# In the eighth attention iteration, the first column pair's fill is issued behind the eight transposes

## The chip, the core and the metric

The kernel runs on one core of one Trainium2 chip. The metric is the device time of one execution in microseconds. All times in this document are in microseconds unless marked otherwise. The engines are TensorE (PE, with its weight loads shown apart as PEld), VectorE (DVE), ScalarE (ACT), GpSimd (POOL) and SyncE (SP, which here only issues DMAs).

## What is computed

The reference is a block of linear attention with a learned feature map, followed by a token-mixing MLP, for one sequence of 2048 tokens and 512 channels. Cut to what matters:

```python
h  = x + attention(layernorm(x))            # 32 heads of 16
h2 = h + mixer(layernorm(h))

# attention: pq, pk = per-head linear maps of q and k
phi_q = concat(softmax(pq), softmax(-pq));  phi_k = likewise
kv = phi_k^T v;  z = sum over tokens of phi_k
o  = (phi_q kv) / (phi_q z + 1e-6);  result = o @ wo

# mixer: works across the 2048 tokens, for every channel
u = gelu(h^T @ w1 + b1)                     # w1: 2048 x 1792
y = u @ w2 + b2                             # w2: 1792 x 2048
```

## The kernel before

The 2048 tokens are 16 tiles of 128. Products that need more than the matmul's own precision are made from three matmuls (`mm3`, L65 to L67): high part by high part, high by low, low by high. `split` (L60, L61) makes such a pair: ScalarE writes the high part, and another engine subtracts it from the source to get the low part.

The first stage makes k, v and q for all tiles. The stage around the change is a loop of 20 iterations, `for it in range(NT + 4)`, that runs the second half of the attention as a pipeline over token tiles. In it the order on TensorE, VectorE, ScalarE and GpSimd is the order in which the code is written, since a manual schedule is in force; only the SP queue's DMAs are placed by the planner, from estimated times. After the loop, until the last stage, the planner also orders the compute engines. What an iteration does, with names and lines:

- `s_pq(it + 1)` (GpSimd, L465) scales the next tile's exponentials `eq` by their weights `w`, which VectorE has made (`s_den`, L456 to L462). `s_ez(it + 3)` (GpSimd, L447) multiplies a later tile's exponentials by `zB`.
- `s_tr(it)` transposes the tile's `eq` with eight TensorE instructions (L532) into the PSUM tile `tn`, which has a single buffer, and ScalarE copies `tn` to `pht` in two halves (L534).
- `s_num`, in even iterations, takes two transposed tiles through `kvB` (L551), also into `tn`; ScalarE and VectorE make the parts `oh` (L557) and `ol` (L562) of it.
- `s_wo(it - 2)` is the output projection, four times `mm3` into `po`. `s_h(it - 2)` (VectorE, L579) adds the residual.
- `s_hn` (ScalarE L593 and L595, then `split`: L60 on ScalarE, L61 on GpSimd) normalizes a tile of the result into `HN`, tile `hs`. `s_rstd` (GpSimd, L590) makes the scale for a later tile. In iteration `it`, `s_hn(it - 4)` is issued: at it = 6 tile 2, at it = 7 tile 3.

TensorE has room in this loop, and the first layer of the mixer is begun in it. The 1792 columns of `w1` are taken in seven column pairs of 256. `fill(p)` adds one token tile to the sums of pair `p`: two times `mm3`, six matmuls into `pu`, the second and fifth of which read the low part of `HN`. Pairs 0 and 1 are filled in the loop by `fills(it)`, pair 1 first. In it = 7 pair 1 takes token tile 1 and pair 0 token tile 2. The weights come in pieces of two token tiles by `fill_load`: a DMA, a high part from ScalarE (L614), and a low part that is put in a list; `flush` has VectorE make the low parts of the list (L606). `flush` is called at the end of each iteration, ahead of that iteration's `fill_load` calls, in which pair 0 comes before pair 1.

In odd iterations the order on TensorE is: the fills, the eight transposes, the output projection. On ScalarE an odd iteration has the two evictions of `tn` ahead of `s_hn`.

After the loop come the remaining fills, the GELUs, and the second mixer layer (L834, L838), which combines blocks of `u` and `w2` into seven products for each step.

Of the kernel before, what the change touches and what calls it, by code (L numbers as in the profile page):

```python
# [28 lines left out]
V_NOT = (0, 1, 11)  # L29
SUMS = 8  # L30
LAG = 5
WARM = 9
EPS = 1e-5

# [2 lines left out]
def block_kernel(ctx: ExitStack, tc: tile.TileContext, x, xT, wT, phic, wo, w1, b1, w2, b2,  # L37
# [25 lines left out]
    def mm3(o, ah, al, bh, bl, first, last):  # L63

        nc.tensor.matmul(o, ah, bh, start=first, stop=False)  # L65
        nc.tensor.matmul(o, ah, bl, start=False, stop=False)  # L66
        nc.tensor.matmul(o, al, bh, start=False, stop=last)  # L67
# [92 lines left out]
    def negate():  # L160

        if MN:
            ev, mx, mn = MN.pop(0)
            nc.gpsimd.tensor_sub(mn, mn, mx)
            nc.gpsimd.tensor_sub(ev[:, :, 1], mn.unsqueeze(3).to_broadcast([P, NPR, 2, DH]), ev[:, :, 0])
# [5 lines left out]
    def run(*lists):  # L171
        for op in turns(*lists):
            op()
# [49 lines left out]
    with tc.tile_pool(name="prep", bufs=1) as prep:  # L223
# [67 lines left out]
        warm = ps_k.tile([P, P], F32, name="pk_ps", tag="pk_ps")  # L291
        for _ in range(WARM):
            nc.tensor.matmul(warm, ones, ones, start=True, stop=True)
# [72 lines left out]
    def q_mm():  # L366
        if q["mm"] < NT:
            PS[q["mm"]] = proj(q["mm"], wqh, wql, ps_q, "pu")
            q["mm"] += 1

    def q_logits(lag):
        n = q["logits"]
        if n < min(NT, q["mm"] - lag + NT * (q["mm"] == NT)):
            EQ[n] = big.tile([P, NG, P], F32, name="eq", tag="big")
            q["logits"] += 1
            return logit_ops(PS[n], EQ[n], n >= len(Q_AT))
        return []

    def q_exp(lag):
        n = q["exp"]  # L380
        if n < min(NT, q["logits"] - len(MN) - lag):
            exps(n, EQ[n])
            q["exp"] += 1
# [61 lines left out]
    def s_ez(t):  # L445
        EZ[t] = az.tile([P, NG, P], F32, name="ez")
        nc.gpsimd.tensor_mul(EZ[t], EQ[t], zB)  # L447

    def s_den(t):


        tz = az.tile([P, NPR, 2, 2], F32, name="tz")
        den = az.tile([P, NPR, 2], F32, name="den")
        W[t] = az.tile([P, NPR, 2, 2], F32, name="w", bufs=3)
        other = SQ[t]
        return [lambda: nc.vector.reduce_sum(tz.rearrange("p g c h -> p (g c h)"), heads(EZ[t]), axis=AX.X),  # L456
                lambda: nc.vector.scalar_tensor_tensor(tz[:, :, 0], other[:, :, 1], 1e-6, tz[:, :, 0],
                                                       op0=ALU.mult, op1=ALU.add),
                lambda: nc.vector.tensor_mul(tz, other, tz),
                lambda: nc.vector.reduce_sum(den, tz.rearrange("p g c h -> p g h c"), axis=AX.X),  # L460
                lambda: nc.vector.reciprocal(den, den),
                lambda: nc.vector.tensor_mul(W[t], other, den.unsqueeze(2).to_broadcast([P, NPR, 2, 2]))]  # L462

    def s_pq(t):
        nc.gpsimd.tensor_mul(heads(EQ[t]), heads(EQ[t]), W[t].rearrange("p g c h -> p (g c h)").unsqueeze(2).to_broadcast([P, 2 * H, DH]))  # L465
# [60 lines left out]
    def s_tr(t):  # L526
        j, i = divmod(t, 2)
        if i == 0:
            PHT[j] = ak.tile([P, NG, 2, P], F32, name="pht", bufs=1)
        ptr = ps_t.tile([P, 2, 4, P], F32, name="tn")  # L530
        for g in range(NG):
            nc.tensor.transpose(ptr[:, g // 4, g % 4, :], EQ[t][:, g, :], ident)  # L532
        for half in range(2):
            nc.scalar.activation(PHT[j][:, half * 4:half * 4 + 4, i, :], ptr[:, half], AF.Copy)  # L534

    def s_kv():

        pt = ps_o.tile([P, 2, P], F32, name="po")
        for b in range(2):
            nc.tensor.transpose(pt[:, b, :], kvS[:, 2 * b:2 * b + 2, :].rearrange("p n f -> p (n f)"), ident)  # L540
        nc.scalar.activation(kvB, pt, AF.Copy)

    def s_num(j):


        pn = ps_t.tile([P, 2, 4, P], F32, name="tn")
        for b in range(2):
            for c in range(4):
                for r in range(2):
                    rows, cols = slice(64 * r, 64 * r + 64), slice(32 * c, 32 * c + 32)  # L550
                    nc.tensor.matmul(pn[cols, r, 2 * b:2 * b + 2, :], kvB[rows, b, cols], PHT[j][rows, 4 * b + c, :, :],  # L551
                                     start=True, stop=True, skip_group_check=True)
        oh = ak.tile([P, 2, 2, 2, P], F32R, name="oh", bufs=1)
        ol = ak.tile([P, 2, 2, 2, P], F32R, name="ol", bufs=1)
        pv = pn.rearrange("p r (b i) s -> p i r b s", i=2)
        for i in range(2):
            nc.scalar.activation(oh[:, i], pv[:, i], AF.Copy)  # L557
        OS[j] = oh, ol, pv

    def s_ol(j):  # L560
        oh, ol, pv = OS[j]
        return [lambda i=i: nc.vector.tensor_sub(ol[:, i], pv[:, i], oh[:, i]) for i in range(2)]  # L562
# [8 lines left out]
    def s_x(t):  # L571
        HT[t] = ak.tile([P, D], F32, name="h", bufs=4)
        nc.sync.dma_start(HT[t], x[t * P:(t + 1) * P, :])
# [18 lines left out]
    def s_hn(t):  # L592
        nc.scalar.activation(VE[t][:, 1:2], VE[t][:, 1:2], AF.Copy, scale=r2[:, t:t + 1])  # L593
        hn = ak.tile([P, D], F32, name="hn")
        nc.scalar.activation(hn, HT[t], AF.Identity, scale=r2[:, t:t + 1], bias=VE[t][:, 1:2])  # L595
        HN[t] = big.tile([P, 2, D], F32R, name="hs", tag="big")
        split(HN[t][:, 0], HN[t][:, 1], hn, nc.gpsimd)
# [5 lines left out]
    def flush():  # L603
        while LATER:
            wl_, raw, wh_ = LATER.pop(0)
            LO.append(nc.vector.tensor_sub(wl_, raw, wh_).ins)  # L606
# [15 lines left out]
    def fill_load(p):  # L622
        if FL[p] < NT:
            WI[p, FL[p]] = stream(w1v, FL[p], 2, p * 256, 256)
            FL[p] += 2

    def fill(p, pool=None):

        t = FN[p]
        FN[p] = t + 1  # L630
        if FL[p] <= t:
            fill_load(p)
        if any(part is WI[p, t - t % 2][1] for part, _, _ in LATER):
            flush()
        if t == 0:
            PU[p] = [pool.tile([P, D], F32, name="pu", tag="pu") for _ in range(2)]
        a, b = WI[p, t - t % 2]
        for c in range(2):
            mm3(PU[p][c], a[:, t % 2, c * P:(c + 1) * P], b[:, t % 2, c * P:(c + 1) * P],
                HN[t][:, 0], HN[t][:, 1], t == 0, t == NT - 1)  # L640

    def fills(it):
        if FN[1] < it - LAG:
            fill(1, ps_q)
        if FN[0] <= it - LAG:
            fill(0, ps_f)

    for it in range(NT + 4):
        even = it % 2 == 0
        if 0 <= it + 1 < NT:  # L650
            s_pq(it + 1)
        if it == 0:
            s_tr(0)
            s_kv()
        if it == 1:
            run(q_logits(0))
            q_mm()
            s_tr(1)
        if it > 1 and even and it <= NT:
            s_num(it // 2 - 1)  # L660
        den = s_den(it + 2) if it + 2 < NT else []
        if it > 1 and even and it <= NT:
            ol = s_ol(it // 2 - 1)
            run(ol[:1] + den[:1] + ol[1:])
            den = den[1:]
        if it < NT:
            s_x(it)
        if it + 3 < NT:
            s_ez(it + 3)
        negate()  # L670
        q_mm()
        fills(it)
        q_exp(0)
        logits = q_logits(1)
        if it >= 4 and even:
            s_hn(it - 4)
        if 3 <= it < NT + 3 and even:
            s_moments(it - 3)
        if it > 1 and even and it - 2 < NT:
            s_wo(it - 2)  # L680
        if 1 < it < NT:
            s_tr(it)
        if it > 1 and not even and it - 2 < NT:
            s_wo(it - 2)
        if it >= 4 and not even:
            s_hn(it - 4)
        if 3 <= it < NT + 3 and not even:
            s_moments(it - 3)
        if 3 <= it < NT + 3:
            s_rstd(it - 3)  # L690
        run(logits + (q_sums(0) if it > 0 else []), den)
        if it > 0:
            negate()
        if not logits:
            flush()
        if 0 <= it - 2 < NT:
            s_h(it - 2)
        flush()
        for p in range(2):
            if it >= LAG - 3 + p and FL[p] <= FN[p] + 2 * (FN[p] > 0):  # L700
                fill_load(p)
# [276 lines left out]
```

## Time and profile before

| | us |
|---|---|
| median of 3 runs | 523.35 (523.15 to 523.65) |
| the profiled execution's own time | 523.61 |
| its span, first to last instruction | 521.8 |
| TensorE busy in the span | 515.2 |
| VectorE, ScalarE, GpSimd busy | 386.0, 282.0, 239.6 |
| granted TensorE clock | 1.000 of full |

A row of a timeline gives the start, the duration, the engine, the source line, the operation, what it writes and reads, shapes and a count; in square brackets, if the engine stood idle before, how long and what released it. Neighbouring instructions of the same kind are merged into one row, whose duration then reaches from the first start to the last end. A matmul's duration contains overlap with its neighbours: while TensorE runs without a break, matmuls of 512 columns start 0.23 apart though each lasts 0.39. Registers, branches and semaphore instructions are not counted as work.

### The profile page before, as it was taken

How to read it: one execution, taken by the hardware profiler on the slowest of the kernel's cores; microseconds unless marked ns; L12 is line 12 of the kernel's file. 1: busy time of each engine (PE TensorE's matmuls, PEld its weight loads, DVE VectorE, ACT ScalarE, POOL GpSimd, SP SyncE). 2: the span in 40 equal slices, each digit the busy share in tenths (PEclk: the TensorE clock that was granted, in tenths of full speed). 3: DMA queues.
4: the chain of work that ended last, by engine and by line, in shares of the span. 5: the costliest groups of instructions: out<-in, count | busy, mean ns of one | idle time of the engine just before them, and what ended most of it. 6: DMA issues, size and time to landing. Idle time of an engine off the chain costs nothing.

```text
span 521.8 us, 8917 instructions
## 1 busy us (share of the span) xinstructions
PE 515.2 (99%) x3379; PEld 435.8 (84%) x3379; DVE 386.0 (74%) x681; ACT 282.0 (54%) x496; POOL 239.6 (46%) x188
## 2 busy tenths in 40 slices
PE   8999999999999999999999999999999999999997
PEld 7888888887877767887788888888889999999997
DVE  6893999986899998773227423725869899988985
ACT  5999853435246876666956423625553424434430
POOL 2479799985999999874425000000002112112220
PEclk9999999999999999999999999999999999999999
DMA  8644211021041324344323354532215686678734
GB/s 299 200 131 121 75 41 38 1 69 36 21 122 49 96 98 125 118 125 137 103 85 118 102 162 155 168 100 82 62 59 109 164 190 147 130 170 180 166 49 81
DMA packets 36298, 58.52 MB, mean 112 GB/s; under 512 B 3744, under 2 KB 19360, under 8 KB 36256
## 3 DMA queue, kind: packets, MB, share of 16 engines
q1 hardware_dynamic: 31936, 51.37, 31.5%
q0 software_dynamic: 4032, 6.42, 9.7%
q8 instruction: 26, 0.43, 0.4%
q10 hardware_dynamic: 288, 0.17, 0.1%
q14 instruction: 16, 0.13, 0.1%
HBM read 46.81 MB, written 11.14 MB: 111 GB/s over the span
## 4 chain that ended last, share of the span: by engine, by line
PE 89%; POOL 7%; DVE 2%; DMA 1%; issue 1%; SPq 0%; ACT 0%; POOLq 0%
PE py L834 16%; PE pu L65 12%; PE pu L66 12%; PE pu L67 11%; PE py L838 10%; PE pv L66 3%; PE pv L67 3%; PE pv L65 3%; PE pk_ps L65 2%; PE pk_ps L67 2%; PE pk_ps L66 2%; POOL ez L447 2%; POOL eq L465 2%; PE po L66 2%; PE po L65 2%; PE po L67 2%
## 5 line engine op out<-in xcount | busy, mean ns | idle before, releaser
L66 PE MATMUL pu<-hs,whi 128*128 128x512 f32 x224 | 87.7, 391 | 1.1 <-POOL hs L61 1.1
L65 PE MATMUL pu<-hs,whi 128*128 128x512 f32 x224 | 87.5, 395 | 0.0
L67 PE MATMUL pu<-hs,wlo 128*128 128x512 f32 x224 | 87.1, 390 | 0.0
L606 DVE TENSOR_TENSOR wlo<-wraw,whi 128x512 fp32r<-128x512 f32 x56 | 43.7, 784 | 53.2 <-ACT whi L614 53.0
L899 POOL DMA_DIRECT2D out<-ot x7 | 6.2, 885 | 151.1 <-DVE ot L895 151.1
L796 ACT ACTIVATE whi<-wraw 128x1792 fp32r<-128x1792 f32 x28 | 47.4, 1701 | 46.0 <-DVE wraw L787 19.8
L805 DVE TENSOR_TENSOR wlo<-wraw,whi 128x1792 fp32r<-128x1792 f32 x28 | 56.5, 2021 | 11.7 <-PE py L838 9.4
L614 ACT ACTIVATE whi<-wraw 128x512 fp32r<-128x512 f32 x56 | 34.9, 628 | 49.6 <-PE pu L66 45.3
L65 PEld LDWEIGHTS pu<-hs,whi 128*128 128x128 f32 x224 | 42.1, 188 | 10.7 <-issue 2.5
L66 PEld LDWEIGHTS pu<-hs,whi 128*128 128x128 f32 x224 | 42.1, 188 | 10.4 <-POOL hs L61 2.1
L834 PE MATMUL py<-uf,whi 128*128 128x512 f32 x175 | 49.8, 395 | 0.0
L67 PEld LDWEIGHTS pu<-hs,wlo 128*128 128x128 f32 x224 | 42.1, 188 | 8.7
L447 POOL TENSOR_TENSOR ez<-eq,zB 128x1024 f32<-128x1024 f32 x16 | 38.3, 2398 | 4.4 <-ACT zB L494 4.4
L838 PE MATMUL py<-uf,whi 128*128 128x256 f32 x210 | 39.1, 283 | 0.0
L200 POOL TENSOR_TENSOR pk<-pk,sk 128x1024 f32<-128x1024 f32 x16 | 31.0, 1940 | 7.6 <-DVE sk L199 5.1
L534 ACT ACTIVATE pht<-tn 128x512 f32<-128x512 f32 x32 | 17.4, 595 | 30.2 <-PE tn L532 30.2
L465 POOL TENSOR_TENSOR eq<-eq,w 128x1024 f32<-128x1024 f32 x16 | 32.2, 2015 | 1.3 <-DVE w L462 1.3
L838 PEld LDWEIGHTS py<-uf,whi 128*128 128x128 f32 x210 | 32.8, 192 | 0.0
L834 PEld LDWEIGHTS py<-uf,wlo 128*128 128x128 f32 x175 | 28.5, 189 | 5.0
L61 POOL TENSOR_TENSOR hs<-hn,hs 128x512 fp32r<-128x512 f32 x16 | 21.6, 1349 | 23.7 <-ACT hs L60 23.7
L204 POOL TENSOR_TENSOR zacc<-zacc,pk 128x1024 f32<-128x1024 f32 x13 | 31.3, 2405 | 0.6
L834 PEld LDWEIGHTS py<-uf,whi 128*128 128x128 f32 x175 | 29.1, 190 | 2.7
(179 smaller groups left out, 1331.9 us busy)
## 6 DMA issues: line engine op xcount, KB each, us to landing
wraw<-in_w SPq DMA_DIRECT2D x56, 256.0 KB, 2.8
wraw<-in_w SPq DMA_DIRECT2D x28, 512.0 KB, 4.4
xraw<-in_xT SPq DMA_DIRECT2D x16, 256.0 KB, 3.0
xh<-in_x SPq DMA_DIRECT2D x16, 256.0 KB, 2.7
h<-in_x SPq DMA_DIRECT2D x16, 256.0 KB, 2.7
out<-h SPq DMA_DIRECT2D x16, 256.0 KB, 2.6
out<-ot POOLq DMA_DIRECT2D x14, 256.0 KB, 4.7
wraw<-in_wT SPq DMA_DIRECT2D x12, 256.0 KB, 5.2
```

Of the source, the lines that this page charges most:

```text
L65: nc.tensor.matmul(o, ah, bh, start=first, stop=False)
L66: nc.tensor.matmul(o, ah, bl, start=False, stop=False)
L67: nc.tensor.matmul(o, al, bh, start=False, stop=last)
L204: nc.gpsimd.tensor_add(zacc, zacc, PK[t])
L447: nc.gpsimd.tensor_mul(EZ[t], EQ[t], zB)
L465: nc.gpsimd.tensor_mul(heads(EQ[t]), heads(EQ[t]), W[t].rearrange("p g c h -> p (g c h)").unsqueeze(2).to_broadcast([P, 2 * H, DH]))
L606: LO.append(nc.vector.tensor_sub(wl_, raw, wh_).ins)
L614: nc.scalar.activation(wh_, raw, AF.Copy)
L796: nc.scalar.activation(WH[g], RAW[g], AF.Copy)
L805: nc.vector.tensor_sub(wl_, RAW[g], WH[g])
L834: nc.tensor.matmul(o, w, u, start=p == 0 and not low, stop=p == NP - 1, skip_group_check=True)
L838: nc.tensor.matmul(bank[bk][:, half], AW[sp, p][x][:, a], UB[p, b][:, y], start=p == 0 and half == 0 and i == 0, stop=p == NP - 1 and i == ...
```

## The change

Only in the iteration with it = 7 (`BEHIND`), the fill of pair 0 is not issued in `fills` but behind `s_tr`. TensorE's order there becomes: the fill of pair 1, the eight transposes, the fill of pair 0, the output projection. All other iterations keep their order.

```diff
+BEHIND = 7
...
-    def fills(it):
+    def fills(it, both):
         if FN[1] < it - LAG:
             fill(1, ps_q)
+        if both:
+            fill_last(it)
+
+    def fill_last(it):
         if FN[0] <= it - LAG:
             fill(0, ps_f)
...
-        fills(it)
+        fills(it, it != BEHIND)
         q_exp(0)
...
         if 1 < it < NT:
             s_tr(it)
+        if it == BEHIND:
+            fill_last(it)
         if it > 1 and not even and it - 2 < NT:
             s_wo(it - 2)
```

## The prediction

> **What bounds the kernel now.** I read the page first, then the list of waits of TensorE over the whole span, then the timeline of each engine around the eighth iteration of the attention loop (it = 7), and last the timeline of older places where VectorE and GpSimd had met in the same way.
>
> ```profile
> span 521.8 us, 8917 instructions
> PE 515.2 (99%) x3379; PEld 435.8 (84%) x3379; DVE 386.0 (74%) x681; ACT 282.0 (54%) x496; POOL 239.6 (46%) x188
> ...
> PE 89%; POOL 7%; DVE 2%; DMA 1%; issue 1%; SPq 0%; ACT 0%; POOLq 0%
> ```
>
> TensorE is busy for 99% of the span, and it is 89% of the chain that ended last. So what counts is whether TensorE gets through its list sooner; a faster engine beside it is worth something only where TensorE waits for it. The waits of TensorE (waiter, waited for, us in total, times, longest) say where that is:
>
> ```profile
> PE pu L66 <- POOL hs L61: 1.1, 1, 1.1
> PE pk_ps L293 <- DVE eps L56: 1.1, 1, 1.1
> PE pv L273 <- DVE wraw L263: 0.7, 1, 0.7
> ```
>
> The second and third rows are of warm-up and weight folding at the start. The first is the one wait of a fill, and it lies exactly where the change is made. TensorE's timeline, with its neighbourhood to the middle of the next iteration:
>
> ```profile
> 187.34 0.39 PE L65 MATMUL pu<-hs,whi 128*128 128x512 f32 x1
> 188.88 0.50 PE L66 MATMUL pu<-hs,whi 128*128 128x512 f32 x1 [1.15 <-POOL hs L61]
> 189.21 0.40 PE L67 MATMUL pu<-hs,wlo 128*128 128x512 f32 x1
> ...
> 190.15 1.04 PE L532 MATMUL tn<-ident,eq 128*128 128x128 f32 x8
> 190.94 0.48 PE L65 MATMUL po<-woh,oh 128*128 128x512 f32 x1
> 191.26 0.39 PE L66 MATMUL po<-wol,oh 128*128 128x512 f32 x1
> ...
> 193.87 1.09 PE L551 MATMUL tn<-pht,kvB 64*32 64x256 f32 x32
> 194.89 0.50 PE L65 MATMUL pu<-hs,whi 128*128 128x512 f32 x1
> 195.23 0.40 PE L66 MATMUL pu<-hs,whi 128*128 128x512 f32 x1
> 195.47 0.39 PE L67 MATMUL pu<-hs,wlo 128*128 128x512 f32 x1
> 195.69 0.40 PE L65 MATMUL pu<-hs,whi 128*128 128x512 f32 x1
> ```
>
> The fill of pair 0 (token tile 2) starts at 187.34. Its second matmul needs the low part of the normalized tile 2 from GpSimd and stands until 188.88. Then come the rest of the fill, the eight transposes at 190.15 (0.79 until the next form starts), the output projection of tile 5 at 190.94, the numerators at 193.87, and from 194.89 the fill of pair 1 of it = 8, whose third matmul (195.47) is the first to use the low weight part of that pair's second load.
>
> **The change, part by part.** Only the place of six matmuls in TensorE's list changes. No instruction is added, removed or sent to another engine; the fill neither starts a load nor flushes a low part here, because its load was made in it = 5 and its low part computed at the end of it = 6. So no DMA and no queue is touched by it directly.
>
> *What the transposes need at 187.34.* Two things: their exponentials, scaled by GpSimd (L465), and the bank `tn`, emptied by ScalarE (L534).
>
> ```profile
> 186.66 0.59 ACT L534 ACTIVATE pht<-tn 128x512 f32<-128x512 f32 x1
> 187.13 1.15 ACT L614 ACTIVATE whi<-wraw 128x512 fp32r<-128x512 f32 x2
> 188.17 1.15 ACT L176 ACTIVATE eq<-eq,r 128x1024 f32<-128x1024 f32 x1
> ...
> 191.23 1.09 ACT L534 ACTIVATE pht<-tn 128x512 f32<-128x512 f32 x2 [1.91 <-PE tn L532]
> ...
> 193.37 0.63 ACT L60 ACTIVATE hs<-hn 128x512 fp32r<-128x512 f32 x1
> ```
>
> ```profile
> 182.86 1.94 POOL L465 TENSOR_TENSOR eq<-eq,w 128x1024 f32<-128x1024 f32 x1
> 184.75 2.38 POOL L447 TENSOR_TENSOR ez<-eq,zB 128x1024 f32<-128x1024 f32 x1
> 187.10 1.72 POOL L61 TENSOR_TENSOR hs<-hn,hs 128x512 fp32r<-128x512 f32 x1
> 188.79 0.54 POOL L590 TENSOR_TENSOR r<-ve,mhalf 128x1 f32<-128x1 f32 x1
> ...
> 191.20 2.40 POOL L447 TENSOR_TENSOR ez<-eq,zB 128x1024 f32<-128x1024 f32 x1
> 194.08 1.81 POOL L61 TENSOR_TENSOR hs<-hn,hs 128x512 fp32r<-128x512 f32 x1 [0.49 <-ACT hs L60]
> ```
>
> The scaled tile is done at 182.86 + 1.94 = 184.80 and the bank is empty at 186.66 + 0.59 = 187.25. Both are there, the second by only 0.09.
>
> *The gain.* The transposes run from 187.34 to 188.13. The fill's first matmul follows at 188.13, and the second could start 0.32 later (as 190.94 to 191.26 after transposes), at 188.45. Its operand still ends at 187.10 + 1.72 = 188.82, so it starts at 188.88 as before, and the wait shrinks to 0.43. The fill then ends at 190.15 as before, but the output projection starts there instead of at 190.94: 0.79 gained. Between matmuls of one form the spacing is 0.23 instead of 0.32, another 0.09. TensorE is 0.88 ahead: numerators at 192.99, fill of pair 1 at 194.01, its third matmul due at 194.59.
>
> *What is late next.* That third matmul needs a low part that VectorE computes in the flush at the end of it = 7. In this flush two subtractions (L606) stand back to back: first pair 0's, then pair 1's. The first row below is the first alone, the second row the two merged:
>
> ```profile
> 186.63 1.05 DVE L606 TENSOR_TENSOR wlo<-wraw,whi 128x512 fp32r<-128x512 f32 x1
> ...
> 191.93 2.22 DVE L606 TENSOR_TENSOR wlo<-wraw,whi 128x512 fp32r<-128x512 f32 x1
> ...
> 191.93 2.82 DVE L606 TENSOR_TENSOR wlo<-wraw,whi 128x512 fp32r<-128x512 f32 x2
> ...
> 196.79 0.69 DVE L562 TENSOR_TENSOR ol<-tn,oh 128x512 fp32r<-128x512 f32 x1 [1.44 <-ACT oh L557]
> ...
> 201.84 0.68 DVE L606 TENSOR_TENSOR wlo<-wraw,whi 128x512 fp32r<-128x512 f32 x1
> ```
>
> The first is done at 194.15, the second at 194.75. So even with nothing else changed, TensorE would start the third matmul at 194.75 + 0.06 = 194.81 (0.06 is what lies between 188.82 and 188.88) and the fourth 0.33 later (as 188.88 to 189.21) at 195.14, against 195.69. Of the 0.88 only 0.55 is left.
>
> But something else does change. Alone such a subtraction takes 0.68 (the row at 201.84). The one at 186.63 took 1.05 and ended at 187.68, which is 0.55 after GpSimd's L447 ended (184.75 + 2.38 = 187.13); the one at 191.93 took 2.22 and ended 0.55 after the next L447 (191.20 + 2.40 = 193.60). It works the other way too: GpSimd's L61 at 187.10 and at 194.08 took 1.72 and 1.81, where undisturbed it takes 1.27:
>
> ```profile
> 200.64 1.27 POOL L61 TENSOR_TENSOR hs<-hn,hs 128x512 fp32r<-128x512 f32 x1
> ```
>
> Both times it ended 1.14 after the subtraction that was in its way. The two engines exclude each other for these operations.
>
> In the kernel before, the second subtraction met no waiting GpSimd, because GpSimd was idle from 193.60 to 194.08, waiting for ScalarE's high part of tile 3 (L60). ScalarE was late because its evictions of `tn` waited 1.91 for the transposes, until 191.23. With the transposes over at 188.13 those evictions start when the exponential ends, 188.17 + 1.15 = 189.32, which is 1.91 earlier; the scale that follows them needs L590, done at 189.33. So the high part ends at 194.00 - 1.91 = 192.09, and GpSimd can send off L61 when L447 ends, at 193.60, about half a microsecond before VectorE sends off the second subtraction (at 194.75 - 0.68 = 194.07, shortly before the first ends). Who goes first then? The nearest precedent has two back-to-back subtraction-like operations of VectorE and a GpSimd operation that arrives between them:
>
> ```profile
> 123.19 0.68 DVE L485 TENSOR_TENSOR zacc<-zacc,pk 128x512 f32<-128x512 f32 x1
> ...
> 123.19 2.15 DVE L485 TENSOR_TENSOR zacc<-zacc,pk 128x512 f32<-128x512 f32 x2
> ...
> 123.45 1.35 POOL L165 TENSOR_TENSOR eq<-mn,eq 128x512 f32<-128x512 f32 x1 [0.42 <-DVE eq L150]
> ...
> 181.83 1.06 POOL L165 TENSOR_TENSOR eq<-mn,eq 128x512 f32<-128x512 f32 x1
> ```
>
> GpSimd's operation, which takes 1.06 undisturbed, waited for the first of them, then ran to 124.80, and VectorE's second ended at 125.34, 0.54 after it: the waiting engine got its turn and the back-to-back successor waited. I take this row, since it has the same pattern. Then L61 ends at 194.15 + 1.14 = 195.29, the second subtraction at 195.29 + 0.55 = 195.84, TensorE's third matmul starts at 195.90 and its fourth at 196.23, against 195.69. **The sum is 0.54 later than before**: 0.88 gained, 1.42 lost.
>
> The Trainium skill, page "SBUF — State Buffer", section "Who interferes with whom", says that a VectorE instruction with two SBUF inputs contends with a GpSimd instruction that reads SBUF, that issue order decides, and that the second fully blocks until the first has finished. By it the order is the one that I take, but with whole durations put end to end (194.15 + 1.27 + 0.68) the second subtraction would end at 196.10 and the sum would be 0.80; the rows show that the blocked operation needs only 0.55 after the release, so the trace differs in size.
>
> *After that.* VectorE goes on from 195.84 with work that before followed a wait of 1.44 (the row at 196.79), GpSimd and ScalarE are at or ahead of their former times, and TensorE is behind its own. Whoever feeds it has more room than before, and after 188.88 TensorE waited for nobody. So the 0.54 neither grows nor is absorbed, and stays to the end.
>
> The profiled execution took 523.61 (span 521.8 and 1.8 around it), 0.26 over the median 523.35. On its own time the sum is 524.15; on the median 523.89, so 523.9.
>
> **The rivals.** What a measurement of this kernel can tell from no change is about 0.2%, 1.05 us; the forecast itself lies within that.
>
> 1. *VectorE keeps its turn.* If the second subtraction goes ahead of L61, 0.55 is gained: 522.8. For it: at 194.07 the second subtraction did follow the first at once, with L61 sent off at 194.08. Against it: the row at 123.45. If moreover the low part were not waited for at all, the full 0.88: 522.5.
>
> 2. *GpSimd takes the first turn too (slower).* The place is 193.60, where L447 ends, VectorE has waited since 191.93 and L61 is ready. It decides if L61 gets in there: L61 ends at 193.60 + 1.27 = 194.87, the first subtraction at 195.42. The small GpSimd operation L590 is then also ahead of the second subtraction. Blocked, it ends 0.41 after the one in its way:
>
> ```profile
> 201.88 1.05 POOL L590 TENSOR_TENSOR r<-ve,mhalf 128x1 f32<-128x1 f32 x1
> ```
>
> (201.84 + 0.68 = 202.52, and 201.88 + 1.05 = 202.93), so at 195.83; the second subtraction ends at 196.38, TensorE's fourth matmul starts at 196.77, and the loss is 1.08: 524.4. Against it: at 187.13 VectorE had waited for L447 and went ahead of an L61 that was ready.
>
> 3. *The transposes do not move up.* With only 0.09 between the emptied bank and 187.34, a release that reaches TensorE later than I read it takes its delay from the remaining 0.43 first; only if it came a whole 1.2 later would nothing be gained, and ScalarE would be no earlier either: 523.35. Nothing shows such a delay.
>
> 4. *The part behind the loop is laid out otherwise.* Its order is set by the planner from estimated times, and the SP queue's in the loop too. A shifted estimate can swap loads or low parts there. From rows before I can bound this only by the waits of that stage, none, and by the largest wait of the list, 1.1 either way: 522.2 to 524.5, and with the 0.54 up to 525.0.
>
> **How the numbers follow.** Forecast 0.60, of which 0.05 for a further small wait that carries it beyond 0.2%; rival 1 0.14 with part of the gain and 0.04 with all; rival 2 0.09; rival 3 0.03; rival 4 0.10 (0.06 slower, 0.04 faster). Slower by over 0.2%: 0.05 + 0.09 + 0.06 = 0.20. Faster by over 0.2%: 0.04, from rival 4 alone. Within: 0.76. The range takes in the forecast, rival 1's part gain, rival 2 and rival 3, with 0.1 to 0.2 at the ends for the scatter of the runs (523.15 to 523.65): 522.7 to 524.6; the full gain and rival 4 are left out.
>
> **What would show it.** In the profile after, the transposes start at about 187.3 and the fill's wait for `hs` is about 0.4. The evictions of `tn` start near 189.3 instead of 191.23. L61 of tile 3 starts at about 193.6 and lasts about 1.7; the second L606 lasts about 1.8 instead of 0.6; and TensorE has a new wait, L67 for `wlo`, of about 1.3. If that wait is 0.2 to 0.3, rival 1 is right; if the first L606 ends near 195.4, rival 2. A wait of TensorE anywhere later than 197, or an order behind the loop that differs, would make the forecast wrong.

## The result, and the profile after

The changed kernel takes 523.90 (median of 14 runs, 523.31 to 524.80), the kernel before 523.07 (14 runs, 522.74 to 523.65). The ratio is 1.0016, with a 95% interval of 1.0008 to 1.0023: 0.4 to 1.2 us slower, by the interval and 523.07. It is no gain, and a small loss.

The two profiled executions give the same span, 521.8. They differ in their beginning as well: the wait of 0.7 for `wraw` that stands in the list of before is absent in the list of after (variation of the start, where the two kernels are alike), and TensorE is 0.59 ahead when it comes to the eighth iteration. So the change is read from a stretch that begins and ends on TensorE itself: from the point where the sixth matmul of pair 1's fill is behind (187.34 in the kernel before) to the fourth matmul of the next fill of pair 1 (195.69). It takes 8.35 before.

Every line behind the edit has moved down in the source, those cited here from the first functions by one: L62 here is L61 of before, L448 is L447, L607 is L606, L533 is L532, and the three matmuls are L66 to L68.

The first three rows of the list of TensorE's waits in the changed kernel (waiter, waited for, us in total, times, longest):

```profile
PE pu L68 <- DVE wlo L607: 1.2, 1, 1.2
PE pk_ps L294 <- DVE eps L57: 1.1, 1, 1.1
PE pu L67 <- POOL hs L62: 0.2, 1, 0.2
```

The wait for `hs` has gone from 1.1 to 0.2, and a wait of 1.2 for a low weight part has come in. The timeline of the changed kernel, TensorE first, then ScalarE, GpSimd and VectorE:

```profile
186.75 1.06 PE L533 MATMUL tn<-ident,eq 128*128 128x128 f32 x8
187.57 0.48 PE L66 MATMUL pu<-hs,whi 128*128 128x512 f32 x1
188.29 0.50 PE L67 MATMUL pu<-hs,whi 128*128 128x512 f32 x1 [0.24 <-POOL hs L62]
...
189.56 0.39 PE L66 MATMUL po<-woh,oh 128*128 128x512 f32 x1
...
192.38 1.09 PE L552 MATMUL tn<-pht,kvB 64*32 64x256 f32 x32
...
193.74 0.40 PE L67 MATMUL pu<-hs,whi 128*128 128x512 f32 x1
195.29 0.50 PE L68 MATMUL pu<-hs,wlo 128*128 128x512 f32 x1 [1.16 <-DVE wlo L607]
195.63 0.40 PE L66 MATMUL pu<-hs,whi 128*128 128x512 f32 x1
...
518.28 0.28 PE L845 MATMUL py<-uf,wlo 128*128 128x256 f32 x1
...
188.62 1.08 ACT L535 ACTIVATE pht<-tn 128x512 f32<-128x512 f32 x2
...
190.76 0.64 ACT L61 ACTIVATE hs<-hn 128x512 fp32r<-128x512 f32 x1
...
190.61 2.40 POOL L448 TENSOR_TENSOR ez<-eq,zB 128x1024 f32<-128x1024 f32 x1
192.96 1.73 POOL L62 TENSOR_TENSOR hs<-hn,hs 128x512 fp32r<-128x512 f32 x1
...
191.33 2.22 DVE L607 TENSOR_TENSOR wlo<-wraw,whi 128x512 fp32r<-128x512 f32 x1
...
191.33 3.90 DVE L607 TENSOR_TENSOR wlo<-wraw,whi 128x512 fp32r<-128x512 f32 x2
```

Read in the order of cause and effect: the transposes start at 186.75, at once. From the fill's second matmul to the numerators it is now 192.38 - 188.29 = 4.09, where it was 193.87 - 188.88 = 4.99: 0.90 gained. The evictions start at 188.62 and wait for nothing, and the high part of tile 3 is ready at 191.40. So L62 is sent off at 192.96 without an idle stretch. VectorE's first subtraction ends at 193.55, L62 at 194.69, and the second subtraction only at 195.23, 1.68 after the first, where it was 0.60 before. TensorE takes the new low part at 195.29. The stretch takes 195.63 - 186.75 = 8.88, which is 0.53 more than before. From there to TensorE's last matmul of the program it is 322.65 in both kernels (195.63 to 518.28, and 195.69 to 518.34 in the kernel before), so the loss is neither made good nor increased. The last matmul in the kernel before:

```profile
518.34 0.28 PE L838 MATMUL py<-uf,wlo 128*128 128x256 f32 x1
```

The instructions of VectorE, ScalarE, GpSimd and SyncE stand in the same order in both traces; on TensorE only the six matmuls have moved.

### The profile page after: what moved, and what is told of

Read it like the earlier page. It is cut to its first block, busy times and chain, and to the rows that moved or that the text cites. A ratio compares the mean times of both kernels' runs of the same rounds, so it can differ in the third digit from the quotient of the medians.

```text
span 521.8 us, 8917 instructions
## 1 busy us (share of the span) xinstructions
PE 515.6 (99%) x3379; PEld 435.5 (83%) x3379; DVE 387.1 (74%) x681; ACT 282.1 (54%) x496; POOL 239.9 (46%) x188
## 4 chain that ended last, share of the span: by engine, by line
PE 91%; DVE 6%; DMA 1%; issue 1%; ACT 1%; SPq 0%; DVEq 0%; ACTq 0%
PE py L841 16%; PE pu L66 12%; PE pu L68 12%; PE pu L67 12%; PE py L845 10%; PE pv L67 3%; PE pv L68 3%; PE pv L66 3%; PE pk_ps L66 2%; PE pk_ps L67 2%; PE pk_ps L68 2%; PE po L67 2%; PE po L68 2%; PE po L66 2%; PE tn L533 2%; PE kvp L213 2%
## 5 line engine op out<-in xcount | busy, mean ns | idle before, releaser
L68 PE MATMUL pu<-hs,wlo 128*128 128x512 f32 x224 | 87.2, 390 | 1.2 <-DVE wlo L607 1.2
L66 PE MATMUL pu<-hs,whi 128*128 128x512 f32 x224 | 87.5, 395 | 0.0
L607 DVE TENSOR_TENSOR wlo<-wraw,whi 128x512 fp32r<-128x512 f32 x56 | 45.0, 806 | 53.3 <-ACT whi L615 53.0
L66 PEld LDWEIGHTS pu<-hs,whi 128*128 128x128 f32 x224 | 42.1, 188 | 10.8 <-issue 2.5
L68 PEld LDWEIGHTS pu<-hs,wlo 128*128 128x128 f32 x224 | 42.1, 188 | 10.3 <-DVE wlo L607 1.6
L448 POOL TENSOR_TENSOR ez<-eq,zB 128x1024 f32<-128x1024 f32 x16 | 38.3, 2398 | 4.4 <-ACT zB L495 4.4
L62 POOL TENSOR_TENSOR hs<-hn,hs 128x512 fp32r<-128x512 f32 x16 | 21.5, 1344 | 23.9 <-ACT hs L61 23.9
```

## The experiments

The theory: the move gains 0.88 and sends ScalarE's high part of tile 3 off early; with that GpSimd gets its turn between the two low parts, and the second, which TensorE wants first, comes 1.1 late. The rivals are in the expectations.

**1. Pair 1's low part first.** Into the changed kernel:

```diff
+        if it == 7:
+            LATER.reverse()
         if not logits:
             flush()
```

> The changed kernel, with one more edit: in the flush at the end of it = 7, VectorE makes pair 1's low part first and pair 0's second. The theory (the 0.88 gained is lost because GpSimd's L62 of tile 3 gets its turn ahead of pair 1's low part) expects that pair 1's low part ends at about 193.4 on the changed kernel's clock, before it is wanted at 193.97, so that the wait of 1.16 for wlo vanishes, no other wait of over 0.1 comes in its place, and the fourth matmul of that fill starts 1.4 earlier than in the changed kernel: 0.9 faster than the kernel before, ratio 0.998. The rival (another producer, such as oh, ol or hs, is as late as the low part) expects that the wait turns up under another name within it = 8 and the ratio is 0.9995 to 1.001.

Measured: 522.18 (11 runs, kernel before 523.00), ratio 0.9986, interval 0.9977 to 0.9994. The list of waits has one row of a fill left; then the timeline:

```profile
PE pu L67 <- POOL hs L62: 0.3, 1, 0.3
```

```profile
186.74 1.06 PE L533 MATMUL tn<-ident,eq 128*128 128x128 f32 x8
...
193.76 0.40 PE L67 MATMUL pu<-hs,whi 128*128 128x512 f32 x1
194.00 0.39 PE L68 MATMUL pu<-hs,wlo 128*128 128x512 f32 x1
194.22 0.40 PE L66 MATMUL pu<-hs,whi 128*128 128x512 f32 x1
...
191.35 3.92 DVE L607 TENSOR_TENSOR wlo<-wraw,whi 128x512 fp32r<-128x512 f32 x2
```

The two subtractions still need 3.92 together, so GpSimd gets in between as in the changed kernel; but what is late now is pair 0's part, which is used an iteration later. The third matmul follows the second by 0.24, without a wait, and nothing else in the iteration takes the wait's place. The stretch takes 194.22 - 186.74 = 7.48, 1.40 less than in the changed kernel and 0.87 less than before. This is the version that is better than both.

**2. The same swap in the kernel before.**

> The kernel before with the same swap of the two low parts. The theory expects no change: in the kernel before pair 1's low part was there 0.7 before it was wanted, so ratio 1.000 within 0.0005 and the wait of 1.1 for hs as before. The rival (pair 1's low part first is worth something by itself) expects 0.998.

Measured: 523.18 (11 runs, kernel before 523.00), ratio 1.0003, interval 0.9994 to 1.0012. The interval is wider than the 0.0005 of the expectation, so the timeline has to show it:

```profile
187.06 0.39 PE L65 MATMUL pu<-hs,whi 128*128 128x512 f32 x1
...
195.41 0.40 PE L65 MATMUL pu<-hs,whi 128*128 128x512 f32 x1
...
193.80 1.81 POOL L61 TENSOR_TENSOR hs<-hn,hs 128x512 fp32r<-128x512 f32 x1 [0.49 <-ACT hs L60]
...
191.65 2.81 DVE L606 TENSOR_TENSOR wlo<-wraw,whi 128x512 fp32r<-128x512 f32 x2
```

The stretch takes 8.35 as before, TensorE's wait for `hs` is 1.16 (1.15 before), and the two subtractions take 2.81 together, with GpSimd's L61 behind them. The swap is worth nothing by itself; it is worth 1.40 where GpSimd gets in between.

**3. The high part of tile 3 sent off later.** Into the changed kernel, on ScalarE:

```diff
+        if it == 7:
+            s_moments(it - 3)
+            for _ in range(2):
+                nc.scalar.activation(ak.tile([P, D], F32, name="hj", bufs=1), HT[4], AF.Copy)
         if it >= 4 and not even:
             s_hn(it - 4)
-        if 3 <= it < NT + 3 and not even:
+        if 3 <= it < NT + 3 and not even and it != 7:
             s_moments(it - 3)
```

With this edit the planner also puts one load of `x` two places later in the SP queue; the tile is wanted two iterations later.

> The changed kernel with more work on ScalarE: in it = 7 the moments of tile 4 and two extra copies of 512 columns (results unused) stand ahead of the normalization of tile 3, so that its high part ends about 2.3 later, near 193.7 on the changed kernel's clock. The theory expects that L62 of tile 3 is then sent off after VectorE's second subtraction (193.30), that this takes about 0.7 and ends near 194.0, that TensorE's wait for wlo shrinks from 1.16 to about 0.1, and that the kernel is 0.5 faster than before (ratio 0.999), although ScalarE has 1.1 more to do. The rival (the second low part is late for a reason of its own, as VectorE's place in the flush) expects the wait of 1.2 unchanged and a ratio of 1.001 to 1.002.

Measured: 522.50 (11 runs, kernel before 523.00), ratio 0.9992, interval 0.9983 to 1.0001. The runs alone hardly tell it from no change; the timeline does:

```profile
186.73 1.06 PE L533 MATMUL tn<-ident,eq 128*128 128x128 f32 x8
...
194.20 0.50 PE L68 MATMUL pu<-hs,wlo 128*128 128x512 f32 x1
194.53 0.39 PE L66 MATMUL pu<-hs,whi 128*128 128x512 f32 x1
...
193.91 1.38 POOL L62 TENSOR_TENSOR hs<-hn,hs 128x512 fp32r<-128x512 f32 x1 [0.92 <-ACT hs L61]
...
191.31 2.83 DVE L607 TENSOR_TENSOR wlo<-wraw,whi 128x512 fp32r<-128x512 f32 x2
```

GpSimd stands idle again, for 0.92. L62 is sent off at 193.91, behind the second subtraction (194.14 - 0.68 = 193.46; the expectation had 193.30), and both subtractions are done after 2.83, at 194.14. The stretch takes 7.80: 0.55 less than before, 1.08 less than in the changed kernel, with more work on ScalarE. Work added on ScalarE made the kernel faster than the changed one (the intervals of the two ratios, 0.9983 to 1.0001 and 1.0008 to 1.0023, do not meet), because it kept GpSimd from getting in.

**4. A smaller delay.** As 3, but only the two copies ahead of `s_hn`; the moments stay in their place.

> The changed kernel with only two extra copies of 512 columns (results unused) on ScalarE ahead of the normalization of tile 3 in it = 7, the moments left in their place. They move the end of the high part by about 1.05, from 191.4 to near 192.4 on the changed kernel's clock. The theory expects that nothing changes against the changed kernel: L62 is held by L448 until 192.8 anyway, so it is still sent off ahead of VectorE's second subtraction (193.30), that one lasts 1.75 and the wait for wlo is 1.1 to 1.2; ratio 1.001 to 1.002 to the kernel before. The rival (work added on ScalarE shifts the engines gradually, and the gain of the experiment with the later high part came from that) expects about half of that gain: a wait for wlo of about 0.6 and a ratio near 1.000.

Measured: 523.66 (11 runs, kernel before 523.19), ratio 1.0007, interval 0.9998 to 1.0015. The interval reaches both the theory's 1.001 and no change, so the timeline has to decide:

```profile
186.86 1.06 PE L533 MATMUL tn<-ident,eq 128*128 128x128 f32 x8
...
195.38 0.50 PE L68 MATMUL pu<-hs,wlo 128*128 128x512 f32 x1 [1.16 <-DVE wlo L607]
195.71 0.40 PE L66 MATMUL pu<-hs,whi 128*128 128x512 f32 x1
...
192.06 0.63 ACT L61 ACTIVATE hs<-hn 128x512 fp32r<-128x512 f32 x1
...
190.69 2.40 POOL L448 TENSOR_TENSOR ez<-eq,zB 128x1024 f32<-128x1024 f32 x1
193.04 1.73 POOL L62 TENSOR_TENSOR hs<-hn,hs 128x512 fp32r<-128x512 f32 x1
...
191.41 3.90 DVE L607 TENSOR_TENSOR wlo<-wraw,whi 128x512 fp32r<-128x512 f32 x2
```

The high part is ready at 192.69, against 191.40 in the changed kernel, but L62 is sent off behind L448 as there, and the wait is 1.16 again. The stretch takes 8.85. So the first 1.29 of the delay on ScalarE has no effect, where the rival expected half the gain: L448 holds L62 until 193.04 all the same. What counts is when L62 is sent off. At 193.04 the loss is there and at 193.91 it is gone; how it goes in between no run shows.

**5. The early high part alone, with no matmul moved.** Into the kernel before, on ScalarE:

```diff
-        if it >= 4 and even:
+        if it >= 4 and (even or it == 7):
             s_hn(it - 4)
...
-        if it >= 4 and not even:
+        if it >= 4 and not even and it != 7:
             s_hn(it - 4)
```

> The kernel before, TensorE's order untouched; only on ScalarE, in it = 7, the normalization of tile 3 stands ahead of the two evictions of tn, so that its high part is ready near 191 instead of 194.0. The theory expects the loss without the move: L61 of tile 3 is sent off at 193.6 and lasts about 1.7, pair 1's low part ends about 1.1 later (195.8), TensorE has both the old wait of 1.1 for hs and a new one of 0.2 to 0.4 for wlo, and the kernel is 0.5 to 0.7 slower than before (ratio 1.001). The rival (the loss comes from the moved matmuls themselves) expects 1.000 and no wait for wlo.

Measured: 523.80 (11 runs, kernel before 523.00), ratio 1.0011, interval 1.0003 to 1.0020. List of waits, then the timeline:

```profile
PE pu L66 <- POOL hs L61: 1.1, 1, 1.1
...
PE pu L67 <- DVE wlo L606: 0.3, 1, 0.3
```

```profile
186.97 0.39 PE L65 MATMUL pu<-hs,whi 128*128 128x512 f32 x1
...
195.52 0.50 PE L67 MATMUL pu<-hs,wlo 128*128 128x512 f32 x1 [0.28 <-DVE wlo L606]
195.86 0.40 PE L65 MATMUL pu<-hs,whi 128*128 128x512 f32 x1
...
193.18 1.74 POOL L61 TENSOR_TENSOR hs<-hn,hs 128x512 fp32r<-128x512 f32 x1
...
191.56 3.91 DVE L606 TENSOR_TENSOR wlo<-wraw,whi 128x512 fp32r<-128x512 f32 x2
```

The old wait stays, the new one comes, and the stretch takes 8.89. That is 0.54 more than before, against 0.53 in the changed kernel, with TensorE's order untouched. The loss is the same, because in both the low part's end sets the time: whatever TensorE had gained before is spent waiting.

**6. The move where TensorE waits for nothing.** In the changed kernel `BEHIND = 9` in place of 7.

> The same move two iterations later only: pair 0's fill behind the transposes in it = 9, it = 7 as in the kernel before. There the fill waits for nothing, so there is nothing to gain, and the flush of it = 9 has a single subtraction, so there is no second one to be overtaken. The theory expects 1.000 within 0.0005, the old wait of 1.1 for hs in it = 7 and no wait of TensorE in it = 9 and it = 10. The rival (the move itself costs or brings something, by the changes between matmul forms) expects 0.1 to 0.9 either way in the time from it = 9 to it = 10.

Measured: 523.19 (11 runs, kernel before 523.19), ratio 0.9999, interval 0.9990 to 1.0008. The list of waits and the timeline, from the transposes of it = 8 to the numerators of it = 10:

```profile
PE pu L67 <- POOL hs L62: 1.1, 1, 1.1
```

```profile
200.55 1.04 PE L533 MATMUL tn<-ident,eq 128*128 128x128 f32 x8
...
202.81 1.06 PE L533 MATMUL tn<-ident,eq 128*128 128x128 f32 x8
203.63 0.49 PE L66 MATMUL pu<-hs,whi 128*128 128x512 f32 x1
203.96 0.39 PE L67 MATMUL pu<-hs,whi 128*128 128x512 f32 x1
...
207.95 1.09 PE L552 MATMUL tn<-pht,kvB 64*32 64x256 f32 x32
```

And the same ends in the kernel before:

```profile
200.47 1.03 PE L532 MATMUL tn<-ident,eq 128*128 128x128 f32 x8
...
207.78 1.09 PE L551 MATMUL tn<-pht,kvB 64*32 64x256 f32 x32
```

It is 7.40 against 7.31: no wait, and 0.09 more on TensorE. That is at the edge of the rival's smallest value, in one profile, and too little for the runs. So the move has next to no price or worth of its own; it depends on the wait that it fills.

## Why the prediction was right

- **The transposes could move up.** They started at 186.75, at the end of pair 1's fill. The margin of 0.09 held.
- **The gain of 0.88** measured 0.90 from the fill's second matmul to the numerators. The wait left was forecast as 0.43 between starts; the list has 0.24, since it counts idle time from the end of the matmul before. Between starts it is 188.29 - 187.57 - 0.32 = 0.40; the transposes took 0.82 until the next form, not 0.79, and the wait absorbed that. Of the gain, the 0.09 from the spacing of equal matmuls came only because here the slower start behind the transposes lies inside the wait: in experiment 6, with no wait there, this gain is absent and the move costs 0.09.
- **The early L61** was forecast to be sent off at 193.60, with L447's end, and to last about 1.7; it was sent off as L448 ended (192.96 against 190.61 + 2.40 = 193.01, which is 193.60 less the 0.59 by which the clocks differ) and lasted 1.73.
- **GpSimd's turn ahead of the second subtraction**, taken from one row of another stage, was right: L62 ended 1.14 after the first subtraction, and the second 0.54 after L62, as reckoned (1.14 and 0.55). Experiment 5 has this step alone with its price of 0.54, and experiments 3 and 4 have it absent and present with the time of sending off. The Trainium skill's rule (page "SBUF — State Buffer", section "Who interferes with whom") that issue order decides agrees with all of these. Its full blocking of the later one would make the second subtraction end 0.68 after GpSimd; the measured end is 0.54 to 0.55 after it in the changed kernel and in experiments 1, 4 and 5, as the prediction had it from the rows.
- **The new wait** was forecast as about 1.3 between starts; it is 195.29 - 193.74 - 0.23 = 1.32, and 1.16 as idle time.
- **The sum of 0.54** is 0.53 in the stretch, and it stays. The median of 523.90 agrees with 523.9 only by the chance of the base, though: the kernel before has come down from 523.35 (3 runs) to 523.07 (14 runs), and the ratio says 0.84 (0.42 to 1.20), in which the 0.53 lies. The remaining 0.3 need not be anything: experiments 4 and 5, whose stretches lose 0.50 and 0.54, have ratios of 1.0007 and 1.0011, and in the eight profiles of this document the stretch begins anywhere from 186.73 to 187.46, where none of the edits has acted yet.
- **The rivals.** That VectorE keeps its turn was priced at 0.55 gained; experiment 3 made that case, and its stretch is 0.55 shorter. That GpSimd takes even the first turn happened in no run, the changed kernel included. The planner left the order behind the loop alone.

## What to carry to other kernels

When a wait is filled by moving work up, follow what the moved work releases, engine by engine, until it meets someone: here early transposes released ScalarE, ScalarE released GpSimd, and GpSimd took a turn from VectorE, whose result TensorE wanted next. Two operations that exclude each other deserve an order that puts the urgent one first; with that order the same move gains 0.87 in the stretch instead of losing 0.53. And if an engine's idle time keeps a resource free for another, filling that idle time has a price.

## What the runs showed of the hardware that was not expected

How sharp the turn is. In the kernel before, the second subtraction (191.93 + 2.82 - 0.68 = 194.07) was sent off only 0.01 ahead of GpSimd's L61 (194.08), both before the first had ended, and it went first; experiment 2 has the same with 193.78 (191.65 + 2.81 - 0.68) against 193.80. In the changed kernel L62 was about 0.5 ahead (192.96, against 193.55 less the 0.08 by which the second is sent off before the first ends) and went first.

Experiment 6 has the same meeting in it = 7, where its order is that of the kernel before:

```profile
192.02 2.82 DVE L607 TENSOR_TENSOR wlo<-wraw,whi 128x512 fp32r<-128x512 f32 x2
...
194.16 1.83 POOL L62 TENSOR_TENSOR hs<-hn,hs 128x512 fp32r<-128x512 f32 x1 [0.47 <-ACT ve L586]
```

The two were sent off together, at 194.16 (192.02 + 2.82 - 0.68), and VectorE's went first here too. The smallest lead shown here with which GpSimd went first is that of the prediction's precedent: sent off at 123.45 against 123.19 + 0.68 - 0.08 = 123.79, so 0.34 ahead. So the turn changes somewhere between a lead of 0 and one of 0.34. Whether the kernel before was some hundredths away from the loss or some tenths is not known. Nor do these rows fit engines that merely take turns, unless GpSimd needs longer to ask than the 0.07 to 0.08 that was left between its sending off and the end of VectorE's first subtraction.
